# Three first factors formed by 256 tokens at a time in one plain block of a retention and bilinear feed-forward kernel

## The chip, the cores and the metric

The kernel runs on one core of a Trainium2 chip. Five engines work side by side, each with its own instructions, and meet at semaphores: TensorE (PE in the profile, with its weight loads as PEld), VectorE (DVE), ScalarE (ACT), GpSimd (POOL) and SyncE (SP), which here issues transfers. The metric is the device time of one execution in microseconds, and the median of the runs is compared.

## The reference

Retention (linear attention with a decay per head) over 8 batches of 576 positions with 8 heads of 64, and then a bilinear feed-forward layer on its 4608 rows:

```python
scores = scale * np.matmul(q, k.transpose(0, 1, 3, 2))
ret = scores * Dmat[None, :, :, :]
x = np.matmul(ret, v)
...
a = x @ w_a
b = x @ w_b
return (a * b @ w_out).astype(np.float32)
```

`Dmat` is `gamma ** (i - j)` at and below the diagonal and zero above it. The width of x is 512, that of a and b 1536.

## The kernel before

The 4608 tokens go through the feed-forward layer in blocks: 512, 256, 256 and then seven of 512. `ffn_block` forms one block. The 1536 columns of a and b are 12 factors of 128. For each factor F, four matmuls over the four quarters of the width (`NC` = 4) give pa (L1394, weights `wa_sb`) in one PSUM bank of 128 x 512, ScalarE copies it to ha in bf16 (L1405), four more give pb (L1412, weights `wb_sb`), and VectorE multiplies both into hT (L1417). Each of these matmuls has a weight load of its own. Banks come from `ps_ffn`, a ring of four tiles with the tag "ab".

The blocks differ. The first four are plain and end in `po` (L1438). The block that starts at token 1536 (`256 * MIXED`) forms its 12 factors in the plain loop too, but its output product is `rows_mixed` (L1047, tiles m), which works with seven products of sums in place of eight (`wo_sums`, `row_sums` at L981). The four after it, from token 2048, run `middle_layer`: factors 0 to 3 from seven products of 256 columns each in place of eight (L1227, tiles lm, ls and la), factors 4 to 11 plain (pa and pb at L1284, ha at L1294, the product at L1297). The last block runs `last_layer`.

The retention of the tokens that come later is done in between, by `stretch`: four groups of 32 small matmuls of 64 x 64 (states L763, keys into states L664, scores L735, scores with values L776). Each goes to a quarter of the array, so four are under way at once. Such a stretch is put into TensorE's order between two factors, where a cost count reaches a due time; in the block of tokens 2048 that is once behind the factors 0 to 3 and once between pb of factor 10 and pa of factor 11.

Operands for a stretch come by transfers that SyncE issues (q, k and v by 256 KB), casts on GpSimd and transposing transfers. TensorE's order is that of the program text. `ps_ffn` gives banks out in turn, so pb of factor 11 in a middle block takes the bank that pb of factor 10 had, with two kv tiles of the stretch and pa of factor 11 between them:

```
4512 L1284 Matmult pb<-xT,wb_sb 128x512 [waits DVE_49]
...
4518 L1284 Matmult pb<-xT,wb_sb 128x512
4519 L763 Ldweights states
4520 L763 Matmult o_3646<-qkT_3260,states 64x64 [waits PE_49]
...
4774 L776 Matmult o_3646<-sT_3491,vb_2921 64x64
4775 L1284 Ldweights wa_sb
4776 L1284 Matmult pa<-xT,wa_sb 128x512
...
4783 L1284 Ldweights wb_sb
4784 L1284 Matmult pb<-xT,wb_sb 128x512 [waits DVE_49]
```

These are rows of the list of TensorE's instructions in the program's order, in the block of tokens 2048. It has 7888 rows; some 20 that only wait on a semaphore are not counted in it.

Of the kernel before, what the change touches and what calls it, by code (L numbers as in the profile page):

```python
# [18 lines left out]
def kernel(  # L19
# [10 lines left out]
    nc = tc.nc  # L30
# [5 lines left out]
    NC = DM // 128  # L36
# [11 lines left out]
    MIXED = 6  # L48
# [44 lines left out]
    def pools_mixed():  # L93

        if not late:
            early.close()
            for name, bufs in (("hsum", 1), ("straight", 2),
                               ("crossed", 2), ("less", 2),
                               ("combo", 1), ("rows", 1)):
                late[name] = early.enter_context(  # L100
                    tc.tile_pool(name=name, bufs=bufs))
# [21 lines left out]
    wa_sb = big.tile([128, NC, DFF], BF16)  # L123
# [7 lines left out]
    def x_of(t0, n):  # L131

        b0 = 0
        for n_b in blocks:
            if t0 < b0 + n_b:
                break
            b0 += n_b
        if b0 not in x_tiles:
            x_tiles[b0] = x_pool.tile([128, HP, 512], BF16, tag="x", name="xT")
        return x_tiles[b0][:, :, t0 - b0:t0 - b0 + n]  # L140
# [168 lines left out]
    def pop():  # L309
        if later:  # L310
            later.pop(0)()
# [3 lines left out]
    def work(budget, up_to=2):  # L315
        jobs.sort(key=lambda job: job[0])
        while jobs and jobs[0][0] <= up_to and jobs[0][1] <= budget:
            _, cost, job = jobs.pop(0)
            job()
            budget -= cost  # L320

    def pass_on(count):
        while copies_due and count:
            copies_due.pop(0)()
            count -= 1
# [594 lines left out]
    def begin_with(F, c, m):  # L920
        begun[F, c, m] = True
        nc.tensor.matmul(begun[F][:, 256 * m:256 * m + 256],
                         wa_sb[:, c, F * 128:F * 128 + 128],
                         x_of(256 * m, 256)[:, c], start=(c == m == 0),
                         stop=(c == NC - 1), skip_group_check=True)
# [77 lines left out]
    def store_formed():  # L1003
        while formed:
            store_mixed(*formed.pop(0))
# [319 lines left out]
    def last_layer(tok0, xT, hT, sums):  # L1325

        quarter, after = layer_mixed(tok0, xT, hT)
        has = {}
        for i, (way, at) in enumerate(ORDER):
            done = None  # L1330
            if way in ("a", "b"):
                F = at
                p1 = ps_ffn.tile([128, 512], FP32, tag="ab", name="p" + way)
                for c in range(NC):
                    w = wa_sb if way == "a" else wb_sb
                    nc.tensor.matmul(p1, w[:, c, F * 128:F * 128 + 128],
                                     xT[:, c], start=(c == 0),
                                     stop=(c == NC - 1))
                    yield 1, False
                if way == "a":  # L1340
                    has[F] = ha_pool.tile([128, 512], BF16, tag="ha",
                                          name="ha")
                    nc.scalar.copy(has[F], p1)
                else:
                    nc.vector.tensor_tensor(hT[:, F], has[F], p1, op=ALU.mult)
                    if F % 2:
                        done = F // 2
            else:
                yield from quarter(at, way)
                after(at, way)  # L1350
                if way == 4:
                    done = at
            if i == 3:
                store_formed()
            if done is not None:
                jobs.extend(row_sums(hT, sums, done, done + 1, SHARED))
            work(SHARE[way])
        work(math.inf, 1)

    def ffn_block(tb, tok0, n, runs):  # L1360

        xT = x_of(tok0, n)
        hT = h_pool.tile([128, NF, 512], BF16, tag="h", name="hT")
        if tok0 >= 256 * MIXED:
            pools_mixed()
            sums = late["hsum"].tile([128, 3, NF // 2, 2, 128], BF16, tag="hsum",
                                  name="hsum")
        f0 = 0
        if tok0 == NTOK - 512:
            yield from last_layer(tok0, xT, hT, sums)  # L1370
            yield from rows_mixed(tok0, hT, sums)
            return
        if tok0 in MIDDLE:
            yield from middle_layer(tok0, xT, hT, sums)
            yield from rows_mixed(tok0, hT, sums)
            return
        for count in runs:
            has = {}
            if tb == 0 and f0 == 0:
                for c in range(2, NC):  # L1380
                    for F in range(count):
                        begin_with(F, c, 1)
            for F in range(f0, f0 + count):
                fs = slice(F * 128, (F + 1) * 128)
                pa = (begun[F] if tb == 0 and F in begun else
                      ps_ffn.tile([128, 512], FP32, tag="ab", name="pa"))
                for c in range(NC):
                    if tb == 0 and (F, 0, 0) in begun:
                        if (F, c, 1) not in begun:
                            begin_with(F, c, 1)  # L1390
                        if c < NC - 1:
                            yield n / 512, False
                        continue
                    nc.tensor.matmul(pa[:, 0:n], wa_sb[:, c, fs],  # L1394
                                     xT[:, c],
                                     start=(c == 0), stop=(c == NC - 1))
                    if c < NC - 1:
                        yield n / 512, False
                if n == 512 and tb:
                    pop()  # L1400
                pass_on(1)
                if F == 2:
                    store_formed()
                ha = ha_pool.tile([128, 512], BF16, tag="ha", name="ha")
                nc.scalar.copy(ha[:, 0:n], pa[:, 0:n])  # L1405
                has[F] = ha
                yield n / 512, False
            for F in range(f0, f0 + count):
                fs = slice(F * 128, (F + 1) * 128)
                pb = ps_ffn.tile([128, 512], FP32, tag="ab", name="pb")  # L1410
                for c in range(NC):
                    nc.tensor.matmul(pb[:, 0:n], wb_sb[:, c, fs],  # L1412
                                     xT[:, c],
                                     start=(c == 0), stop=(c == NC - 1))
                    if c < NC - 1:
                        yield n / 512, False
                nc.vector.tensor_tensor(hT[:, F, 0:n], has[F][:, 0:n],  # L1417
                                        pb[:, 0:n], op=ALU.mult)
                pop()
                if tok0 >= 256 * MIXED:  # L1420
                    if F == 7:
                        jobs.extend(row_sums(hT, sums, 0, 4))
                    elif F == NF - 1:
                        jobs.extend(row_sums(hT, sums, 4, 6))
                        work(math.inf, 1)
                work(1.0)
                yield n / 512, True
            f0 += count
        if tb == 0:
            yield from rows_together(tok0, hT, (0, 1))  # L1430
        if tok0 >= 256 * MIXED:
            yield from rows_mixed(tok0, hT, sums)
            return
        for u in range(2 if tb == 0 else 0, n // 128):
            osb = half_of(o_pool, u, [DM], FP32, "osb")
            po = ps_ffn.tile([128, 512], FP32, tag="ab", name="po")
            for F in range(NF):
                nc.tensor.matmul(po, hT[:, F, u * 128:(u + 1) * 128],  # L1438
                                 wo_sb[:, F],
                                 start=(F == 0), stop=(F == NF - 1))  # L1440
                if F in (2, 5, 8):
                    pop()
                    work(1.2)
                    pass_on(1)
                if F < NF - 1:
                    yield 1, F % 4 == 3
            if n == 256 or u % 2 == 0:
                nc.scalar.copy(osb, po)
            else:
                nc.vector.tensor_copy(osb, po)  # L1450
            held.append((tok0 // 128 + u, slice(0, DM), osb))
            pop()
            yield 1, True
# [99 lines left out]
    starts, at = {}, 0.0  # L1553
# [96 lines left out]
    at = 0.0  # L1650
# [40 lines left out]
```

## Time and profile before

| what | value |
| --- | --- |
| median of three runs | 315.55 us (315.49 to 316.35) |
| the profiled execution: its time | 315.94 us |
| its span, first to last instruction | 314.2 us |
| TensorE busy, matmuls | 302.9 us (96%), 3910 records |
| GpSimd busy | 203.5 us (65%) |
| VectorE busy | 223.4 us (71%) |
| ScalarE busy | 156.0 us (50%) |
| moved by transfers | 50.97 MB, 162 GB/s |

The block of tokens 1536 forms its factors from 121.1 to 144.6 us of the span. Its pa of the factors 8, 9 and 10 start at 136.4, 138.1 and 139.8 us. The first middle block starts its output product at 177.8 us, the second at 209.7 us.

In an order of time, a row has the start, the length, the engine, the line, the operation with its tiles and shape, the count of instructions merged into it, and in brackets the idle time before it with what ended that. In a list of waits a row has who waited for whom, microseconds in total, how often, and the longest. In a table by stretch a row has a stretch of the span, for each engine its busy time and in brackets its instructions, then the granted clock, the share of the transfer engines and GB/s. Of a transfer queue a row has its packets, megabytes, and the packets' time as a share of the time of 16 engines in the window asked for. A few matmul records are missing from the trace, so a group of four can read x3.

### The profile page before, as it was taken

The page shows a single profiled execution, that of the slowest core. Times are in us where ns is not written, and L with a number is a line of the kernel's source. Part 1 is how long each engine was busy: PE and PEld are TensorE (multiplying, and loading weights), DVE is VectorE, ACT ScalarE, POOL GpSimd, SP SyncE. Part 2 cuts the span into 40 slices and gives each one's busy share as a digit, 9 for nine tenths or more (in the row PEclk, how much of TensorE's full clock was granted, in tenths as well). Part 3 has the DMA queues.
Part 4 walks back from the last instruction along what each step waited for, and adds up shares of the span by engine and source line. Part 5 has one row for each costly group of instructions (what it writes and reads, how often), then busy time and mean ns, then how long its engine had stood idle before and what let it go on. Part 6 is the DMA issues. An engine that isn't in the chain of part 4 may idle for free.

```text
span 314.2 us, 9621 instructions
## 1 busy us (share of the span) xinstructions
PE 302.9 (96%) x3910; PEld 197.6 (63%) x3943; DVE 223.4 (71%) x450; ACT 156.0 (50%) x351; POOL 203.5 (65%) x290
## 2 busy tenths in 40 slices
PE   7899999999999999999999899999999999999994
PEld 3554457768544554547864687468746875687774
DVE  5745337757847664778777786889669968877873
ACT  7755346626435453555446446545634564335530
POOL 3990079675996669775899659985999350035413
PEclk9999999999999999999999999999999999999999
DMA  8999999999999999999999986947703030013004
GB/s 214 257 203 206 251 234 196 192 213 177 210 174 216 213 227 200 230 213 282 197 277 192 180 185 185 191 84 177 212 18 62 20 124 2 2 47 88 3 0 136
DMA packets 144797, 50.97 MB, mean 162 GB/s; under 512 B 126576, under 2 KB 141680, under 8 KB 144752
## 3 DMA queue, kind: packets, MB, share of 16 engines
q1 hardware_dynamic: 138272, 45.10, 70.4%
q0 software_dynamic: 5808, 4.72, 9.5%
q8 instruction: 31, 0.51, 0.7%
q10 hardware_dynamic: 672, 0.52, 0.5%
q14 instruction: 14, 0.11, 0.1%
HBM read 37.75 MB, written 9.44 MB: 150 GB/s over the span
## 4 chain that ended last, share of the span: by engine, by line
PE 88%; DVE 3%; issue 2%; DMA 2%; ACT 2%; SPq 2%; ACTq 0%; DVEq 0%
PE m L1047 16%; PE pb L1412 13%; PE pa L1394 12%; PE po L1438 8%; PE pb L1284 8%; PE pa L1284 8%; PE lm L1227 7%; PE ls L1227 3%; DMA qf<-in_q_dram 2%; SPq L182 2%; PE la L1227 2%; PE po L933 2%; PE sc L735 1%; PE o L763 1%; PE kv L664 1%
## 5 line engine op out<-in xcount | busy, mean ns | idle before, releaser
L1417 DVE TENSOR_TENSOR hT<-ha,pb 128x512 bf16<-128x512 bf16 (+1 forms) x60 | 34.6, 579 | 33.1 <-PE pb L1412 28.4
L1412 PE MATMUL pb<-xT,wb_sb 128*128 128x512 bf16 (+1 forms) x238 | 50.0, 336 | 0.3
L1394 PE MATMUL pa<-xT,wa_sb 128*128 128x512 bf16 (+1 forms) x225 | 47.3, 334 | 0.7 <-issue 0.5
L1071 POOL TENSOR_TENSOR osb<-crossed,straight 128x256 f32<-128x256 f32 x24 | 17.5, 757 | 46.1 <-ACT crossed L1059 35.7
L1405 ACT CAST ha<-pa 128x512 bf16<-128x512 f32 (+1 forms) x60 | 29.9, 500 | 35.0 <-PE pa L1394 32.5
L1412 PEld LDWEIGHTS <-wb_sb 128*128 128x128 bf16 x240 | 23.4, 98 | 18.3 <-issue 0.3
L1284 PE MATMUL pb<-xT,wb_sb 128*128 128x512 bf16 x125 | 32.1, 379 | 1.2 <-DVE sums L688 1.0
L579 POOL TENSOR_TENSOR qkb<-qf,qs 64x512 bf16<-64x512 f32 x24 | 24.8, 1051 | 12.9 <-DMA qf<-in_q_dram 4.9
L616 POOL TENSOR_TENSOR vb<-vf,vs 128x512 bf16<-128x512 f32 x30 | 31.4, 1066 | 2.2 <-DMA vf<-in_v_dram 1.0
L1394 PEld LDWEIGHTS <-wa_sb 128*128 128x128 bf16 x232 | 22.1, 98 | 17.0 <-DVE sums L691 0.2
L1284 PE MATMUL pa<-xT,wa_sb 128*128 128x512 bf16 x119 | 31.4, 379 | 0.7 <-issue 0.3
L1047 PEld LDWEIGHTS <-hT 128*128 128x128 bf16 x288 | 28.1, 98 | 5.0 <-DVE hT L981 0.5
L1294 ACT CAST ha<-pa 128x512 bf16<-128x512 f32 x32 | 18.7, 586 | 24.7 <-PE pa L1284 24.7
L1297 DVE TENSOR_TENSOR hT<-ha,pb 128x512 bf16<-128x512 bf16 x32 | 21.9, 684 | 11.5 <-PE pb L1284 9.5
L609 POOL CAST qkb<-kf 64x256 bf16<-64x256 f32 x60 | 28.4, 500 | 1.5
L1438 PE MATMUL po<-wo_sb,hT 128*128 128x512 bf16 x113 | 26.7, 379 | 0.8 <-issue 0.6
L584 POOL TENSOR_TENSOR qkb<-qf,qs 64x512 bf16<-64x512 f32 x24 | 26.0, 1103 | 0.7
L1047 PE MATMUL m<-wo_sums,hsum 128*128 128x256 bf16 x216 | 25.7, 273 | 0.0
L981 DVE TENSOR_TENSOR hsum<-hT 128x512 bf16<-128x512 bf16 (+2 forms) x51 | 23.6, 495 | 0.5
L605 POOL CAST qkb<-kf 64x512 bf16<-64x512 f32 x30 | 20.3, 675 | 3.7 <-DMA kf<-in_k_dram 2.3
L1047 PEld LDWEIGHTS <-hsum 128*128 128x128 bf16 x216 | 21.1, 98 | 2.5
L1284 PEld LDWEIGHTS <-wb_sb 128*128 128x128 bf16 x128 | 12.3, 98 | 15.5 <-issue 1.3
(159 smaller groups left out, 578.3 us busy)
## 6 DMA issues: line engine op xcount, KB each, us to landing
qf<-in_q_dram SPq DMA_DIRECT2D x32, 256.0 KB, 5.3
vf<-in_v_dram SPq DMA_DIRECT2D x32, 256.0 KB, 4.9
kf<-in_k_dram SPq DMA_DIRECT2D x31, 256.0 KB, 5.0
out_dram<-osb SPq DMA_DIRECT2D x9, 512.0 KB, 3.2
out_dram<-osb SPq DMA_DIRECT2D x22, 128.0 KB, 2.8
wo_sb<-in_moe_w_out_dram POOLq DMA_DIRECT2D x3, 512.0 KB, 15.7
out_dram<-osb SPq DMA_DIRECT2D x6, 256.0 KB, 4.5
qf<-in_q_dram SPq DMA_DIRECT2D x8, 128.0 KB, 3.3
```

The costliest lines, as they stand in the source:

```text
L579: nc.gpsimd.tensor_tensor(per_head(qkb[0:64, Q])[:, hs], per_head(t[0:64])[:, hs], by[0:64, hs].unsqueeze(2).to_broadcast([64, H, D]), op= ...
L584: nc.gpsimd.tensor_tensor(per_head(qkb[64:128, Q])[:, 1 - r::2], per_head(t[64:128])[:, r::2], by[64:128, r::2].unsqueeze(2).to_broadcast( ...
L609: nc.gpsimd.tensor_copy(to[:, :, 1 - r], fro[:, :, r])
L616: nc.gpsimd.tensor_tensor(vb[:, e].rearrange("p (h d) -> p h d", d=D), t[:, e].rearrange("p (h d) -> p h d", d=D), decay[:, at], op=ALU.mult)
L1047: nc.tensor.matmul(to, rows, cols, start=(begins and p == 0), stop=True, skip_group_check=True)
L1227: nc.tensor.matmul(to[:, m], w[:, c], x[:, c], start=(way in (1, 2, 5) and m == c == 0), stop=True, skip_group_check=True)
L1284: nc.tensor.matmul(p1, w[:, c, F * 128:F * 128 + 128], xT[:, c], start=(c == 0), stop=(c == NC - 1))
L1394: nc.tensor.matmul(pa[:, 0:n], wa_sb[:, c, fs], xT[:, c], start=(c == 0), stop=(c == NC - 1))
L1405: nc.scalar.copy(ha[:, 0:n], pa[:, 0:n])
L1412: nc.tensor.matmul(pb[:, 0:n], wb_sb[:, c, fs], xT[:, c], start=(c == 0), stop=(c == NC - 1))
L1417: nc.vector.tensor_tensor(hT[:, F, 0:n], has[F][:, 0:n], pb[:, 0:n], op=ALU.mult)
L1438: nc.tensor.matmul(po, hT[:, F, u * 128:(u + 1) * 128], wo_sb[:, F], start=(F == 0), stop=(F == NF - 1))
```

## The change

In `ffn_block`, the pa of three factors in the block of tokens 1536 are formed by 256 tokens at a time: for each quarter of the width two matmuls on the two halves of the bank, each with its own load of the same weights.

```diff
+    BY_HALVES = [(256 * MIXED, F) for F in (8, 9, 10)]
+
     def ffn_block(tb, tok0, n, runs):
...
-                    nc.tensor.matmul(pa[:, 0:n], wa_sb[:, c, fs],
-                                     xT[:, c],
-                                     start=(c == 0), stop=(c == NC - 1))
+                    width = n // 2 if (tok0, F) in BY_HALVES else n
+                    for at in range(0, n, width):
+                        nc.tensor.matmul(pa[:, at:at + width],
+                                         wa_sb[:, c, fs],
+                                         xT[:, c, at:at + width],
+                                         start=(c == at == 0),
+                                         stop=(c == NC - 1),
+                                         skip_group_check=(width < n))
```

Four loads and four matmuls of a factor become eight and eight: 8 more instructions for each of three factors, 24 in all. The `yield`s that count costs stay as they are, one for each quarter, so the due times of all other work fall where they fell. TensorE's list has 7912 rows, and from the third of these factors on every row stands 24 further on; the lists of the other engines have the same rows in the same order. At the rows of the listing above stands now:

```
4536 L1284 Matmult pb<-xT,wb_sb 128x512 [waits DVE_49]
...
4783 L776 Ldweights vb_2921
4784 L776 Matmult o_3658<-sT_3503,vb_2921 64x64
```

## The prediction

> **What bounds the kernel now.** I read the page first, for the engine that carries the end.
>
> ```profile
> span 314.2 us, 9621 instructions
> PE 302.9 (96%) x3910; PEld 197.6 (63%) x3943; DVE 223.4 (71%) x450; ACT 156.0 (50%) x351; POOL 203.5 (65%) x290
> PEclk9999999999999999999999999999999999999999
> DMA  8999999999999999999999986947703030013004
> q8 instruction: 31, 0.51, 0.7%
> PE 88%; DVE 3%; issue 2%; DMA 2%; ACT 2%; SPq 2%; ACTq 0%; DVEq 0%
> ```
>
> TensorE is busy for 96% of the span at full granted clock and has 88% of the chain that ended last. What costs it time is therefore either an instruction more or a stall. Second comes the list of TensorE's waits, longest first; the first row is the start of the kernel, the second is the only single wait of more than 0.5 us behind it.
>
> ```profile
> PE w L1463 <- DVE idxp_f L227: 1.5, 1, 1.5
> PE pb L1284 <- DVE sums L688: 1.0, 1, 1.0
> ...
> PE pa L1394 <- issue: 0.5, 3, 0.2
> ```
>
> That second wait lies in the block of tokens 2048, just after the changed block. I took TensorE's order of time around it, and then the same place one block later.
>
> ```profile
> 173.51 0.45 PE L763 MATMUL o<-qkT,states 64*64 64x64 bf16 x32
> 173.78 0.44 PE L664 MATMUL kv<-vb,qkb 64*64 64x64 bf16 x32
> 174.04 0.50 PE L735 MATMUL sc<-qkT 64*64 64x64 bf16 x32
> 174.33 0.58 PE L776 MATMUL o<-sT,vb 64*64 64x64 bf16 x32
> 175.08 0.81 PE L1284 MATMUL pa<-xT,wa_sb 128*128 128x512 bf16 x3 [0.16 <-issue]
> 176.91 1.02 PE L1284 MATMUL pb<-xT,wb_sb 128*128 128x512 bf16 x4 [1.03 <-DVE sums L688]
> ```
> ```profile
> 208.14 0.81 PE L1284 MATMUL pa<-xT,wa_sb 128*128 128x512 bf16 x3 [0.16 <-issue]
> 208.79 1.03 PE L1284 MATMUL pb<-xT,wb_sb 128*128 128x512 bf16 x4
> ```
>
> From pa's first shown matmul to pb's it is 0.65 us in the later block and 1.83 us here, so TensorE stands still for 1.18 us (x3 where the program has four is a missing record, and so are the 0.16). The row names VectorE's copy of L688. I asked what pb of factor 11 really needs: the PSUM bank of pb of factor 10, four tiles back in the ring of four (pb 10, two kv, pa 11, pb 11), which the product of L1297 frees.
>
> ```profile
> 168.51 0.69 DVE L1297 TENSOR_TENSOR hT<-ha,pb 128x512 bf16<-128x512 bf16 x1 [1.04 <-PE pb L1284]
> ...
> 170.60 0.69 DVE L1297 TENSOR_TENSOR hT<-ha,pb 128x512 bf16<-128x512 bf16 x1
> ...
> 173.77 0.68 DVE L1297 TENSOR_TENSOR hT<-ha,pb 128x512 bf16<-128x512 bf16 x1
> 174.37 1.49 DVE L981 TENSOR_TENSOR hT<-hT 128x1024 bf16<-128x1024 bf16 x2
> 175.78 0.41 DVE L688 COPY sums<-kv 128x256 f32<-128x256 f32 x1
> ```
>
> That product (173.77) ends at 174.45, before pa 11 even starts, and the copy named ends at 176.19, still 0.72 us before pb goes on. No wait on data explains it. TensorE's own instructions are the other thing that it can lack. The page has 31 packets and 0.51 MB on the instruction queue q8, 16.5 KB each; the program has 7888 rows for TensorE, so a packet is a block of about 254, and I take 256. Four views of transfers follow: the first before the stall, the second from 174.31 to 174.33, the third from 171.2 to 177, the fourth from 175.7 to 179.1.
>
> ```profile
> q1 hardware_dynamic: 6315, 1.58, 124.5%
> q14 instruction: 1, 0.01, 0.5%
> ```
> ```profile
> q8 instruction: 1, 0.02, 396.6%
> ```
> ```profile
> q8 instruction: 1, 0.02, 1.4%
> ```
> ```profile
> q1 hardware_dynamic: 2014, 0.50, 114.0%
> ```
>
> The first runs from 166.9 to 174.3 and has no q8 row; the fourth has none either. One block of TensorE's instructions thus begins to land at 174.32 and takes 1.4% of 16 engines over 5.8 us, 1.3 us: it is there at 175.6. TensorE goes on at 176.91, 1.3 us behind it, about what the news of a landing may cost (an estimate from this one case). And the 256 before were gone quickly, as the busy times by stretch show:
>
> ```profile
> 167.40:174.30 6.90, 6.90 (x122) 3.41 (x122) 5.20 (x8) 4.85 (x10) 6.68 (x8) 1.00 1.33 230
> 173.50:174.80 1.30, 1.30 (x129) 1.27 (x128) 1.30 (x3) 0.16 (x1) 1.26 (x2) 1.00 1.40 229
> 176.20:176.90 0.70, 0.00 (x0) 0.00 (x0) 0.00 (x0) 0.70 (x2) 0.70 (x1) 1.00 0.19 31
> ```
>
> In 1.3 us of the 64x64 products 257 instructions of TensorE go by (x129 and x128), as many as a block holds; in the dense part before, 244 take 6.9 us. The stalled matmul is row 4784 of TensorE's order. If a block begins there, the block before it is rows 4529 to 4783, and the four groups of 64x64 products are rows 4519 to 4774: nearly the whole block is used up in 1.3 us, and the next is asked for too late. I read the stall so: an edge between instruction blocks that falls just behind such a stretch. No other of TensorE's rows shows one.
>
> **The change part by part.** Three pa (factors 8, 9, 10 of the block of tokens 1536) become eight matmuls of 256 columns each in place of four of 512; the program's list has 7912 rows in place of 7888. Nothing else is added or moved on any engine or queue.
>
> ```profile
> 50.52 0.44 PE pa L1394 x4
> ...
> 121.27 0.86 PE pa L1394 x4
> ```
> ```profile
> 144.61 2.78 PE L1047 MATMUL m<-wo_sums,hT 128*128 128x256 bf16 x24
> 147.23 1.47 PE L1047 MATMUL m<-wo_sums,hsum 128*128 128x256 bf16 x12
> ```
> ```profile
> L1394 PEld LDWEIGHTS <-wa_sb 128*128 128x128 bf16 x232 | 22.1, 98 | 17.0 <-DVE sums L691 0.2
> ```
>
> First, the split. At the same line four matmuls of 256 columns take 0.44 us in the chain and four of 512 take 0.86; a long run gives 2.62/24 = 0.109 us each at 256. Eight are 0.87 against 0.86, so three factors cost 0.03 us. The twelve weight loads more, 98 ns each, go beside the matmul before, as they do in that run at a pace of 0.109. Without that cover they would cost 12 x 0.098 = 1.2 us, which I exclude, since the run has a load to each matmul; below nothing it can't go, as the columns are the same. I take 0.03.
>
> Second, the grid. Every later instruction stands 24 rows further on in blocks whose edges stay at the same rows. The edge at row 4784 now falls 24 rows earlier in the work: in the last product group (L776), 14 rows from its end, which TensorE passes at about 174.65. The block before that edge begins 24 rows earlier too, twelve matmuls of 512 columns earlier, for its start lies in the dense part behind pb 9. When is it asked for? No row shows the request. If it goes with TensorE's position, it moves by 12 x 0.216 = 2.6 us. If the sequencer can't read past a matmul whose bank isn't free, it goes with the releases: the product of 170.60 (ends 171.29, frees the bank for pb 10) before; that of 168.51 (ends 169.20, for pb 9) or ScalarE's cast below (ends 168.16, for pa 9) after. That is 2.1 to 3.1 us.
>
> ```profile
> 167.57 0.59 ACT L1294 CAST ha<-pa 128x512 bf16<-128x512 f32 x1 [0.65 <-PE pa L1284]
> ...
> 175.93 0.59 ACT L1294 CAST ha<-pa 128x512 bf16<-128x512 f32 x1 [0.35 <-PE pa L1284]
> ```
>
> So TensorE could go on past the edge at 176.91 - 2.6 = 174.3 (173.8 to 174.8) and comes to it at 174.68 (0.03 later for the split). What is left of the stall is nothing (nothing to 0.1). I take 0.05 for it.
>
> Third, what is late next. With the stall gone pb 11 starts at 175.76, the output products m of L1047 at 176.62. They need the second ScalarE cast above, which ends at 176.52, and VectorE's sums of L981, which end at 175.86: both just in time, as they are one block later where no stall stands. Behind that TensorE waits for nothing worth 0.3 us, so the gain reaches the end.
>
> The sum against the profiled execution: its span of 314.2 - 1.18 + 0.03 + 0.05 = 313.1, and its time of 315.94 (1.74 around the span) becomes 314.84. The median of the three runs, 315.55, is 0.39 below the profiled time; the same 1.10 off it gives **314.45**.
>
> **The rivals.** *It isn't the fetch.* The stall could be something in TensorE's sequencer that belongs to this place in the work, not to a grid. For it: VectorE's row is named, and the fetch and the stall meet in one case only. Against: the bank was free at 174.45, and one block later the same work shows nothing. Then only the split counts: 315.55 + 0.03 = 315.58. [...]
>
> *The fetch doesn't move.* The transfer engines are full from 167.4 to 174.3 (a share of 1.33: packets overlap); if the block is held up by the qf, kf and vf packets queued ahead of it and not asked for late, it still lands at 175.6. TensorE then meets the edge at 174.68, waits to 176.91, and has 14 rows of products and four matmuls of pa still to do (175.73 - 174.65 = 1.08 us): pb 11 starts at 177.99 in place of 176.91, and the kernel is 1.08 us slower, 316.63. It decides from a landing that starts later than 173.2 (174.68 + 1.18 - 0.03 - 1.3 - 1.3), where the gain is used up. Against it: the loads ahead of the fetch run in 256-byte packets without a pause, and the page's transfer row reads 9 nearly all the way to 180 us while TensorE's list has no second wait of this kind.
>
> A new edge behind another 64x64 stretch would be of the same sign; every stretch after this one has its edge 24 rows elsewhere. One block later pb 11 stands 139 rows past an edge and will stand 163 past it, far from both ends.
>
> **How the numbers follow.** The forecast has 0.70, no fetch 0.17, the fetch that doesn't move 0.13. A measurement of this kernel can tell about 0.3% from no change, 0.95 us, and the forecast of 1.10 us is little beyond it: the stall of the unprofiled runs may be somewhat shorter, as their time is. Of the 0.70 I give 0.60 to faster and 0.10 to the same; of the second 0.16 to the same and 0.01 to slower; of the third 0.03 to the same (the wait in part) and 0.10 to slower. That makes 0.60, 0.29, 0.11. The range goes down to 1.18 gained with 0.4 for the spread of the runs (315.49 to 316.35), 313.9, and up over the second case with the beginning of the third, 315.9; the forecast alone would span 314.1 to 314.9.
>
> **What would show it.** Right: pb at L1284 follows pa in 0.65 us in the block of tokens 2048, the wait on the sums copy is gone from the list, the q8 packet that began at 174.32 begins at 171 to 172.6, and the three split factors take 0.87 us each. Wrong: that packet still begins after 173.2; or a gap of about a microsecond inside the L776 group at 174.65; or TensorE again idle between pa and pb; or new waits in later blocks, above all before the m products, that give the microsecond back.

## The result and the profile after

| | median | ratio to before (95% interval) |
| --- | --- | --- |
| before, 22 runs | 315.53 us (314.91 to 317.09) | |
| the change, 22 runs | 314.83 us (314.43 to 316.17) | 0.9974 (0.9961 to 0.9986) |

The change makes the kernel 0.26% faster, 0.82 us by the ratio, with an interval from 0.44 to 1.23. The profiled execution took 314.71 us against 315.94 before. Its page opens with a span 1.2 us shorter, and the q8 queue, which the prediction took for the one of TensorE's instructions, has 31 packets as before:

```profile
span 313.0 us, 9645 instructions
PE 303.0 (97%) x3922; PEld 198.6 (63%) x3955; DVE 224.0 (72%) x450; ACT 156.0 (50%) x351; POOL 202.8 (65%) x290
q8 instruction: 31, 0.51, 0.7%
PE 91%; DVE 2%; DMA 2%; SPq 2%; issue 2%; ACT 1%; DVEq 0%; ACTq 0%
```

TensorE's list of waits in the changed kernel (who waited for whom, us in total, times, longest) has no row of pb at L1284 any more:

```profile
PE w L1470 <- DVE idxp_f L227: 1.5, 1, 1.5
PE po L1445 <- issue: 0.6, 4, 0.2
PE sc L407 <- ACT qkT L393: 0.5, 1, 0.5
```

TensorE's order of time in the block of tokens 2048 of the changed kernel:

```profile
173.63 0.45 PE L763 MATMUL o<-qkT,states 64*64 64x64 bf16 x32
...
174.45 0.47 PE L776 MATMUL o<-sT,vb 64*64 64x64 bf16 x32
175.08 0.81 PE L1284 MATMUL pa<-xT,wa_sb 128*128 128x512 bf16 x3 [0.16 <-issue]
175.73 1.03 PE L1284 MATMUL pb<-xT,wb_sb 128*128 128x512 bf16 x4
176.59 2.78 PE L1047 MATMUL m<-wo_sums,hT 128*128 128x256 bf16 x24
```

From pa to pb it is 0.65 us where it was 1.83 before, the same as one block later. VectorE's order of time in the changed kernel shows that pb did not need the copy of L688 that its wait was put down to:

```profile
173.97 0.68 DVE L1297 TENSOR_TENSOR hT<-ha,pb 128x512 bf16<-128x512 bf16 x1
...
175.97 0.41 DVE L688 COPY sums<-kv 128x256 f32<-128x256 f32 x1
```

The copy of L688 ends at 176.38, and pb began at 175.73 without it. The transfers of the changed kernel between 170.16 and 170.18 us hold the start of a q8 packet, the 18th of the 31, as the one at 174.32 was before:

```profile
q8 instruction: 1, 0.02, 332.5%
```

It begins at 170.17, 4.15 us earlier, and 3.46 us ahead of the stretch of 64x64 products (173.63), where it was 0.81 us behind the stretch's start (173.51).

### The profile page after: what moved, and what is told of

Its sections match the earlier page's. It is cut to its first block, busy times and chain, and to the rows that moved or that the text cites. A ratio compares the mean times of both kernels' runs of the same rounds, so it can differ in the third digit from the quotient of the medians.

```text
span 313.0 us, 9645 instructions
## 1 busy us (share of the span) xinstructions
PE 303.0 (97%) x3922; PEld 198.6 (63%) x3955; DVE 224.0 (72%) x450; ACT 156.0 (50%) x351; POOL 202.8 (65%) x290
## 4 chain that ended last, share of the span: by engine, by line
PE 91%; DVE 2%; DMA 2%; SPq 2%; issue 2%; ACT 1%; DVEq 0%; ACTq 0%
PE m L1047 16%; PE pb L1419 13%; PE pa L1398 12%; PE pb L1284 9%; PE pa L1284 9%; PE po L1445 8%; PE lm L1227 7%; PE ls L1227 3%; DMA qf<-in_q_dram 2%; SPq L182 2%; PE la L1227 2%; PE po L933 2%; PE sc L735 2%; PE o L763 1%; PE kv L664 1%
## 5 line engine op out<-in xcount | busy, mean ns | idle before, releaser
L1398 PEld LDWEIGHTS <-wa_sb 128*128 128x128 bf16 x244 | 23.3, 98 | 16.5 <-DVE sums L691 0.2
L1284 PE MATMUL pb<-xT,wb_sb 128*128 128x512 bf16 x125 | 32.1, 379 | 0.2
L1284 PE MATMUL pa<-xT,wa_sb 128*128 128x512 bf16 x119 | 31.4, 379 | 0.7 <-issue 0.3
L609 POOL CAST qkb<-kf 64x256 bf16<-64x256 f32 x60 | 27.7, 488 | 1.5
L1284 PEld LDWEIGHTS <-wb_sb 128*128 128x128 bf16 x128 | 12.3, 98 | 14.3
```

Of the source, the lines that this page charges most:

```text
L609: nc.gpsimd.tensor_copy(to[:, :, 1 - r], fro[:, :, r])
L1284: nc.tensor.matmul(p1, w[:, c, F * 128:F * 128 + 128], xT[:, c], start=(c == 0), stop=(c == NC - 1))
L1398: nc.tensor.matmul(pa[:, at:at + width], wa_sb[:, c, fs], xT[:, c, at:at + width], start=(c == at == 0), stop=(c == NC - 1), skip_group_ch ...
```

## Is it the grid of 256 instructions?

The grid means here the edges between blocks of 256 instructions, one to a q8 packet: an estimate in the prediction (31 packets and 7888 rows make about 254), which the runs of this section put to the test. Two more profiles of before show how far its stall varies. A whole block of rows more, a third of the change, and the same count at another place tell the grid from the splitting. Each ratio is to the runs of before on the same chip; their median was 315.93 us for the runs of this section and 315.99 us for those of the next, so the medians themselves are not to be compared with 315.53. All edits use the change's own form:

```diff
+                    width = n // 2 if (tok0, F) in A_BY_HALVES else n
+                    for at in range(0, n, width):
+                        nc.tensor.matmul(pa[:, at:at + width],
...
```

and the same for pb with `B_BY_HALVES`; the lists are all that differs, and one that isn't shown is empty.

**The kernel before, again.** No edit.

> The kernel before, profiled once more. If the stall ahead of pb 11 (L1284, block of tokens 2048) hangs on when a block of TensorE's instructions lands, it varies from execution to execution with the q8 packet: pb 11 goes on about 1.3 us behind the packet's end, and the stall may lie anywhere from 0.4 to 1.6 us. If it belongs to this place in the work alone, it is 1.18 us again, whatever the packet does.

315.27 us, span 313.6. TensorE's order of time:

```profile
173.63 0.44 PE L763 MATMUL o<-qkT,states 64*64 64x64 bf16 x32
...
175.08 0.81 PE L1284 MATMUL pa<-xT,wa_sb 128*128 128x512 bf16 x3 [0.16 <-issue]
176.32 1.02 PE L1284 MATMUL pb<-xT,wb_sb 128*128 128x512 bf16 x4 [0.43 <-DVE hT L981]
177.18 1.04 PE L1047 MATMUL m<-wo_sums,hT 128*128 128x256 bf16 x8
```

From pa to pb it is 1.24 us, a stall of 0.59 against 1.18 in the first profile, and another instruction of VectorE is named for it. The packet begins at 173.35, 0.97 us earlier than in the first profile. The packet came earlier and the stall is shorter; in the third profile below the packet is late and the stall long again.

**256 rows more.**

```diff
+    A_BY_HALVES = [(1536, F) for F in range(0, 12)] + [(1024, F) for F in range(4, 12)]
+    B_BY_HALVES = [(1536, F) for F in range(0, 12)]
```

> All 24 pa and pb of the block of tokens 1536 and the pa of factors 4 to 11 of the block of tokens 1024 formed by 256 tokens at a time: 256 rows more ahead of the stall, a whole block of instructions, so the edges fall on the same work as before. Theory of the grid: the stall ahead of pb 11 is back with about 1.2 us, and the kernel is 32 x 0.01 = 0.3 us slower than before (315.8). Rival (the splitting itself, or any change of time ahead of the place, takes the stall away): no stall, 314.7 + 0.2 = about 315.0.

315.68 us, ratio 0.9997 (0.9981 to 1.0013). TensorE's order of time:

```profile
173.99 0.45 PE L763 MATMUL o<-qkT,states 64*64 64x64 bf16 x32
...
175.44 0.81 PE L1284 MATMUL pa<-xT,wa_sb 128*128 128x512 bf16 x3 [0.16 <-issue]
176.09 0.38 PE L1284 MATMUL pb<-xT,wb_sb 128*128 128x512 bf16 x1
176.95 0.82 PE L1284 MATMUL pb<-xT,wb_sb 128*128 128x512 bf16 x3 [0.48 <-issue]
177.61 0.82 PE L1047 MATMUL m<-wo_sums,hT 128*128 128x256 bf16 x6
```

The stall is back: 0.86 us between two starts that are 0.216 apart elsewhere, so 0.64. And it has moved by one matmul: pb's first one runs, and TensorE stands ahead of the second, which waits for nobody. This program has 256 loads and matmuls more and one instruction less that only waits on a semaphore, 255 in all, so with blocks of 256 the edge must fall one instruction later: on the weight load of pb's second matmul in place of pb's first matmul. That is where it falls. Splitting as such takes no stall away, and the size differs from the expected 1.2 as it does between two executions of before.

**8 rows more.**

```diff
+    A_BY_HALVES = [(1536, F) for F in range(8, 9)]
```

> Only the pa of factor 8 split: 8 rows more. The edge falls on the first pa matmul of factor 11. If the request for the block goes with TensorE's position, it comes 8 rows or 0.86 us earlier: TensorE stands about 1.15 us ahead of pa 11 in place of pb 11, and nothing is gained (315.6). If the sequencer's reading is held by unfulfilled waits, the request comes either with the release for pb 10 as before (171.3: TensorE goes on at 176.9 with pa 11, 0.9 us slower, 316.4) or with the one for pb 9 (169.2: no stall, 314.7). If the splitting itself is what helps: about a third of the gain, 315.3.

315.72 us, ratio 0.9998 (0.9981 to 1.0014): a third of the change gains nothing. TensorE's order of time:

```profile
173.96 0.44 PE L763 MATMUL o<-qkT,states 64*64 64x64 bf16 x32
...
174.78 0.47 PE L776 MATMUL o<-sT,vb 64*64 64x64 bf16 x32
176.44 0.81 PE L1284 MATMUL pa<-xT,wa_sb 128*128 128x512 bf16 x3 [1.19 <-issue]
177.09 1.03 PE L1284 MATMUL pb<-xT,wb_sb 128*128 128x512 bf16 x4
```

The stall now stands ahead of pa of factor 11, where the edge falls with 8 rows: from L776 to pa it is 1.66 us in place of the change's 0.63, so 1.03. The packet begins at 173.41. The place is that of the grid, and the size is near the 1.15 that the expectation gave for a request that goes with TensorE's position.

**24 rows at another place.**

```diff
+    B_BY_HALVES = [(1024, F) for F in range(0, 3)]
```

> 24 rows more at another place and in another product: the pb of factors 0 to 2 of the block of tokens 1024, 35 us and more ahead of the changed pa. Theory of the grid: the same as the change, no stall ahead of pb 11, 314.8. Rival (the three pa's place or the banks they use matter): the stall stays, 315.6.

314.96 us, ratio 0.9977 (0.9960 to 0.9995), the change's own within the intervals. One instruction that only waits is gone here too, so 23 are added. TensorE's order of time has no stall:

```profile
175.70 0.81 PE L1284 MATMUL pa<-xT,wa_sb 128*128 128x512 bf16 x3 [0.16 <-issue]
176.35 1.03 PE L1284 MATMUL pb<-xT,wb_sb 128*128 128x512 bf16 x4
```

For this stall neither the block nor pa nor its banks matter; the count of instructions ahead of it does: none with 23 and 24 more, 0.64 us with 255 more.

## How the request moves, and how the runs scatter

**16 rows more.**

```diff
+    A_BY_HALVES = [(1536, F) for F in range(8, 10)]
```

> The pa of factors 8 and 9 split: 16 rows more. The edge falls into the last group of 64x64 products (L776), which TensorE passes at about 174.8. With 8 rows the q8 packet began only 0.2 us earlier against the stretch's start than in the second profile of before, with 24 rows 3.1 us. Held by unfulfilled waits: the next 8 rows bring the request over the wait of pb 10, and the packet begins with the release for pb 9 or pa 10 (169.2 to 169.9) and some 2.1 us, at 171.3 to 172.0: no stall, 314.8. Position alone, in even steps: the packet begins about 0.4 us earlier than in the second profile of before, at 173.0, and TensorE stands some 0.9 us inside the L776 group, 315.9.

314.86 us, ratio 0.9961 (0.9946 to 0.9977). TensorE's order of time:

```profile
174.84 0.45 PE L763 MATMUL o<-qkT,states 64*64 64x64 bf16 x32
...
175.67 0.47 PE L776 MATMUL o<-sT,vb 64*64 64x64 bf16 x32
176.29 0.81 PE L1284 MATMUL pa<-xT,wa_sb 128*128 128x512 bf16 x3 [0.16 <-issue]
176.94 1.03 PE L1284 MATMUL pb<-xT,wb_sb 128*128 128x512 bf16 x4
```

No stall: two thirds of the edit bring the gain. The packet begins at 173.06, but this execution reaches the stretch later, at 174.84, so it is 1.78 us ahead of it. The time is that of the first reading, and the even steps' stall of 0.9 us inside L776 did not come.

**248 rows more.**

```diff
+    A_BY_HALVES = [(1536, F) for F in range(0, 12)] + [(1024, F) for F in range(5, 12)]
+    B_BY_HALVES = [(1536, F) for F in range(0, 12)]
```

> All pa and pb of the block of tokens 1536 and the pa of factors 5 to 11 of the block of tokens 1024 split: 248 rows more, with one instruction that only waits gone, so 9 rows short of a whole block: the edge falls 9 rows later in the work, behind the first output product m of L1047, which TensorE comes to at about 177.0. The block before it begins inside the first 64x64 group, behind the first product there, which waits for TensorE's own results. If unfulfilled waits hold the reading, the request comes only when the stretch starts (173.9), the packet begins at about 176.0, TensorE goes on at 178.6, and stands 1.5 us between the first and second m: 316.2 to 316.6. If only waits on other engines hold it, the request comes at 171.6 and nothing or little stalls: 315.1 to 315.4.

315.35 us, ratio 0.9988 (0.9970 to 1.0007). TensorE's order of time:

```profile
173.88 0.45 PE L763 MATMUL o<-qkT,states 64*64 64x64 bf16 x32
...
176.10 1.03 PE L1284 MATMUL pb<-xT,wb_sb 128*128 128x512 bf16 x4
176.96 1.81 PE L1047 MATMUL m<-wo_sums,hT 128*128 128x256 bf16 x14
```

The packet begins at 174.46, 0.58 behind the stretch's start, and is only just too late for the edge behind the first m. No record is missing here: the 14 products take 0.1 us more than their pace of 0.109 needs, and TensorE's weight loads show where:

```profile
176.75 0.10 PEld L1047 LDWEIGHTS <-hT 128*128 128x128 bf16 x1
177.17 0.22 PEld L1047 LDWEIGHTS <-hT 128*128 128x128 bf16 x3 [0.33 <-issue]
```

The load of the second m starts 0.42 us behind that of the first, where it is 0.22 in before, and holds up its matmul by 0.1 us. That is the instruction on which the edge was expected, 9 rows later in the work than in before. (The L735 products of the stretch take another 0.12 us here, 174.41 to 174.82 where 0.29 us is usual; why is open.) A request that TensorE's own unfulfilled waits hold back would have cost 1.5 us by the expectation's estimate; with 0.1 measured that reading is wrong. The 31 split factors themselves cost some 0.3 us of the time (an estimate, 31 x 0.01), so the ratio stays near 1 though the stall is nearly gone.

**Third profile of before, second of the change.** No edits.

> The kernel before, a third profile. Grid and late landing: pb 11 goes on 1.3 to 1.6 us behind the end of the q8 packet that begins between 173.2 and 174.5, wherever that lies; the stall is between 0.4 and 1.3 us.

316.06 us. TensorE's order of time:

```profile
175.05 0.81 PE L1284 MATMUL pa<-xT,wa_sb 128*128 128x512 bf16 x3 [0.16 <-issue]
177.02 1.02 PE L1284 MATMUL pb<-xT,wb_sb 128*128 128x512 bf16 x4 [1.16 <-DVE sums L688]
```

From pa to pb it is 1.97 us, a stall of 1.32, just above the expected range. The packet begins at 174.17.

> The changed kernel, a second profile: the q8 packet begins between 170 and 172 and TensorE stands nowhere between 173 and 178; what its time has above 314.4 lies elsewhere.

317.92 us, 3.2 us above the first profile of the change, and yet without a stall at the place:

```profile
176.89 0.45 PE L763 MATMUL o<-qkT,states 64*64 64x64 bf16 x32
...
178.35 0.81 PE L1284 MATMUL pa<-xT,wa_sb 128*128 128x512 bf16 x3 [0.16 <-issue]
178.99 1.03 PE L1284 MATMUL pb<-xT,wb_sb 128*128 128x512 bf16 x4
179.86 1.36 PE L1047 MATMUL m<-wo_sums,hT 128*128 128x256 bf16 x11
```

The packet begins at 173.79, later than the 170 to 172 that was expected, as everything here comes some 3.3 us later: the stretch starts at 176.89, and the packet is again 3.10 us ahead of it. The delay lies far ahead of the place. At the kernel's start the list of waits has a row that the first profile lacks:

```profile
PE kv L434 <- ACT vb L379: 1.2, 1, 1.2
```

And from 15 to 20 and from 20 to 24 us the granted clock was 0.84 and 0.77, where the first profile has 1.00 in both; the mean over the execution was 0.993 against 0.998.

All ten profiles together, each number from the starts in TensorE's order of time, the q8 row's window and the span:

| kernel | stretch starts | stretch to first m | packet against stretch | first m to the end |
| --- | --- | --- | --- | --- |
| before, 1st | 173.51 | 4.27 | +0.81 | 136.4 |
| before, 2nd | 173.63 | 3.55 | -0.28 | 136.4 |
| before, 3rd | 173.49 | 4.39 | +0.68 | 136.4 |
| 256 rows | 173.99 | 3.62 | +0.16 | 136.4 |
| 248 rows | 173.88 | 3.08 | +0.58 | 136.5 |
| 8 rows | 173.96 | 3.99 | -0.55 | 136.4 |
| 16 rows | 174.84 | 2.97 | -1.78 | 136.4 |
| the change, 1st | 173.63 | 2.96 | -3.46 | 136.4 |
| the change, 2nd | 176.89 | 2.97 | -3.10 | 136.3 |
| 24 rows elsewhere | 174.25 | 2.96 | -3.39 | 136.4 |

The change's gain is all in the third column, from the stretch to the first m: 4.07 in the mean of before's three profiles against 2.96, 1.1 us. Most of the scatter between executions is in the second column, the start of the stretch, and behind the first m nothing changes but the 0.1 us of the 248 rows.

## Why the prediction held

**The forecast and its size.** Faster by 1.10 us was forecast and 0.82 (0.44 to 1.23) measured; 314.83 lies in the range. For the profiled pair the span of 313.1 came out as 313.0. The term of the stall, 1.18 us from one execution, is 0.59 in the second and 1.32 in the third. That may be why the runs gained less than the profiled pair, as the prediction had said they might, but it isn't shown: the profiles don't tell which share of the 22 runs has which stall, and the interval holds 1.10 too. The chance of 0.60 for more than 0.3% was somewhat high: by the ratio it is 0.26%, with 0.3% inside the interval.

**No wait on data.** Right. With the edge elsewhere pb runs ahead of the copy that was named for its wait.

**The edge at the stalled row.** Right, and to the instruction: one wait-only instruction less moved the stall by one instruction, to the load of pb's second matmul; 8 rows moved it from pb to pa, and 248 rows to the second m. One sentence of the prediction was too strong, that no other of TensorE's rows shows such a stall. Counted by the recorded weight loads (each has one matmul) and the instructions that only wait, the grid has an edge 17 blocks of 256 earlier, in the small products of L520 (64 x 128) at about 15.3 us: in the first profile of before 2169 such loads and 14 such waits stand between the two stalled matmuls, 4352 instructions or 17 x 256, and the packets ahead of the two stalls, at 12.80 and 174.32 us, are the 1st and the 18th of q8. That bears out the 256 of the prediction, where the page gave about 254. The profile with 256 rows shows a stall there:

```profile
15.27 0.30 PE L520 MATMUL o<-sT,vb 64*64 64x128 bf16 x7
15.95 0.55 PE L520 MATMUL o<-sT,vb 64*64 64x128 bf16 x25 [0.39 <-issue]
```

Eight of the ten profiles have this gap, ahead of the same matmul, from 0.11 us between two starts (the first profile of before) to 0.60 (256 rows). TensorE goes on each time 2.4 to 2.6 us behind the start of a q8 packet. The two without it, 16 rows and the second of the change, came there a microsecond later. The change leaves this edge where it was.

**The split at 0.03.** Right. TensorE's order of time in the changed kernel has a split pa and the pb behind it:

```profile
136.53 1.04 PE L1398 MATMUL pa<-xT,wa_sb 128*128 128x256 bf16 x8
137.40 1.03 PE L1419 MATMUL pb<-xT,wb_sb 128*128 128x512 bf16 x4
138.26 1.04 PE L1398 MATMUL pa<-xT,wa_sb 128*128 128x256 bf16 x8
```

0.87 us for a split pa, 0.86 for a pb.

**The request moves by 2.6 us (2.1 to 3.1).** Right in sign, too small: 4.15 in the profiled pair, and 3.7 against the stretch when all profiles of a kind are averaged (+0.40 to -3.32). Nothing hung on it, as the 2.1 would have left a stall of 0.1 at most. At the dense pace of 0.108 us a row the packet should stand at -0.46, -1.3 and -2.2 against the stretch for 8, 16 and 24 rows; it stands at -0.55, -1.78 and -3.32. The three profiles of before lie 1.1 us apart, so the one profile each of 8 and of 16 rows can't tell that reading from the one of releases. The 24 rows, at -3.10 to -3.46 in three profiles, lie beyond even steps. No row shows a request, and what sets its moment stays open, and so does how much of its delay is due to the q, k and v packets on the transfer engines: leaving those loads out was not tried.

**What is late next.** Right: m starts at 176.59 where 176.62 was said, just behind ScalarE's cast.

```profile
175.93 0.59 ACT L1294 CAST ha<-pa 128x512 bf16<-128x512 f32 x1 [0.35 <-PE pa L1284]
```

It ends at 176.52, and 136.4 us follow in both kernels.

**The rivals.** That it isn't the fetch fell with the 8, 248 and 256 rows: the stall stands each time on the instruction on which the grid's edge falls, and a whole block more brings it back to its place but for one instruction. In the first profile of before the block of the packet that begins at 174.32 was missed at 175.73, 1.41 us later. That the fetch doesn't move fell with the first profile of the change; 8 rows show, though, how it would have looked: a stall of 1.03 ahead of pa with nothing gained.

## What to carry to other kernels

A stall of TensorE ahead of an instruction whose semaphores were all met earlier (the copy named here ended 0.72 us before pb went on) may be a missing block of instructions: look whether a packet of the instruction queue landed a microsecond or two before TensorE goes on (here its end lay 1.3 to 1.6 us before), and count TensorE's rows back to the stretch of short matmuls that used up the block (here 257 instructions in 1.3 us). In this kernel 16, 23 and 24 instructions more upstream took the stall away, 8 moved it to pa and 255 brought it back, so a gain or loss of a microsecond after an unrelated edit may be the grid and not the edit: add a whole block of instructions and see whether it comes back. A stretch that uses a block in about a microsecond, as the 1.3 us here, should not fill the block just ahead of an edge; here 16 rows were enough, with which that block began a few rows ahead of the stretch in place of inside it.

## What the runs showed of the hardware that was not expected

From the start of the late packet to TensorE's next instruction it took 2.59 us (176.91 - 174.32), 2.97 (176.32 - 173.35), 2.85 (177.02 - 174.17) and, with 256 and 248 rows, 2.80 (176.95 - 174.15) and 2.71 (177.17 - 174.46). With the 2.4 to 2.6 at L520 that is 2.4 to 3.0, while TensorE waited from 0.1 us to 1.3. The stretch of 64x64 products uses as many instructions as a block holds (257 from 173.50 to 174.80 in the first profile of before) in 1.3 us, about half of that. In the ten profiles the six packets that began from 0.55 us ahead of the stretch's start to 0.81 behind it were too late, and the four that began 1.78 us or more ahead of it were in time.
